# Attention in a fused kernel: the short query block of 64 rows moves from the end to the start

## The chip, the cores and the metric

The kernel runs on one core of a Trainium2 chip. The metric is the device time of one execution in microseconds (us). The program computes causal attention, a mixture of experts and a gated MLP in one launch; the change touches only the attention.

## What is computed

```python
scores = q @ k.T / sqrt(64)                       # 4 batches x 8 heads, S = 576, D = 64
cum    = cumsum(maximum(s, 0))
scores = where(causal, -1e9, scores + minimum(-(cum[:, None] - cum[None, :]), 0))
p      = exp(scores - rowmax(scores))
out    = (p / (p.sum(-1) + 1e-9)) @ v
x      = out as 2304 tokens x 512                  # then: top-1 of 8 experts, 512 -> 1024 -> 512
y      = (silu(norm(x) @ w_gate) * (norm(x) @ w_val)) @ w_out      # 512 -> 1536 -> 512
```

The term that depends on the row alone falls out of a softmax, so the kernel adds only the column's cumulative sum, less the one in the middle. Everything is float32.

## The kernel before

**Pairs.** The 32 heads are handled as 16 pairs, p0 to p15. The two heads of a pair lie on the upper and the lower 64 rows of TensorE's array, so their matmuls run side by side.

**Query blocks.** A pair has five blocks of queries. Blocks 0 to 3 hold 128 queries each and see 128, 256, 384 and 512 columns of keys for each head (`s_start`, `s_mm`). Block 4 holds the last 64 queries of both heads, one head above the other on 128 partitions; a block-diagonal copy of q (`q_diag`, L284, on GpSimd) makes that one matmul, over 576 keys in two halves of 288 (L341).

**Steps of a pair.** TensorE writes scores into PSUM (tiles `s` and `sm`). VectorE reads them, adds the bias, scales, and takes the row's extreme in one pass (`reduced`, L298). ScalarE takes the exponential with the row sums (`s_exp`, L354). TensorE transposes the probabilities in 25 squares of 128 x 128, seven groups t0 to t6 (`t_mm`, L373), ScalarE copies them to `pt` (L406), and TensorE multiplies by v (`pv_mm`: `pvy` L419, `pvx` L423) and, with the gate's weights, forms the output tile `tl` (`o_mm`, L447). PSUM has eight banks in one rotation, shared by all of these tiles: a tile waits until the reader of the eighth tile before it is done.

**Bias.** `load_bias` sends each pair's cumulative sums to all partitions by DMA: `sums`, two transfers of 256 KB, and `cm`, two of 144 KB, for the block of two heads. From p2 on the causal mask is not a matmul but part of the bias, and GpSimd prepares it (`mask_sums`): once per pair for both heads (n = 0: L249 and L250, 512 and 256 columns) and, once VectorE has read block 1, once for each head (n = 1, 2: L253, 256 columns each), into the same buffer. Block 2 is reduced after that, as the last of the four wide ones (`TURN`).

**Order.** A list `plan` holds the steps with a key 10*p + POS. TensorE, ScalarE, VectorE and SyncE take them in the order of the keys. GpSimd does not: its order is made by the framework's planner, which takes what it reckons to be ready and, of several ready ones, the earlier in the program. `in_turn` adds explicit orders: what it wraps comes after the last instruction in `k.turn`. The program order of `mask_sums` is

```python
S=[0.11, 0.2, 0.81, 0.83, 5.96],      # keys of the five score steps, in the order TURN
MASK = -9.7                           # mask_sums(p + 1, 0) stands at 10 * p + 0.3
mask_sums(k, p, 1 + h)                # inside s_mm(p, 1), so at 10 * p + 0.2
```

so `mask_sums(p + 1, 0)` follows `mask_sums(p, 1)` and `(p, 2)`, and is tied behind them by `in_turn`. SyncE issues the loads of q, k, bias and v for later pairs, and from p1 to p3 the eight `prefill` transfers, which write filler rows to the experts' token buffer (`xs<-zrow`).

Of the kernel before, what the change touches and what calls it, by code (L numbers as in the profile page):

```python
# [2063 lines left out]
```

## Time and profile before

| | us |
|---|---|
| median of three runs (838.82 to 839.22) | 839.19 |
| the profiled execution | 838.61 |
| its span | 836.9 |
| TensorE busy | 816.7 (98%) |
| VectorE busy | 639.6 (76%) |
| ScalarE busy | 461.9 (55%) |
| GpSimd busy | 227.0 (27%) |

The span runs from the first to the last instruction. In the views PE is TensorE, DVE is VectorE, ACT is ScalarE, POOL is GpSimd and SP is SyncE; L298 is line 298 of the kernel, and PEclk is the granted clock of TensorE, with 1.00 for 2.4 GHz and 0.50 for 1.2 GHz. The attention fills about 5 to 180 us; a pair begins with its first `s` matmul and takes about 10.4 us, while its later steps overlap the next pairs.

### The profile page before, as it was taken

What the parts mean: (1) busy time and instruction counts of PE and PEld (TensorE: products, weight loads), DVE (VectorE), ACT (ScalarE), POOL (GpSimd) and SP (SyncE); (2) the same over time, 40 slices, a digit from 0 to 9 for tenths busy, and PEclk for the clock granted to TensorE, in tenths of its full rate; (3) what the DMA queues carried; (4) which work ended last, traced back from release to release, by engine and by line L of the source; (5) the groups of instructions that cost most, each with busy time, mean ns of one, the idle gap of its engine ahead of it and who ended that gap; (6) DMA issues with size and microseconds to landing.
All of it is one profiled execution on the core that took longest, in us unless ns stands there. A gap on an engine that the chain in (4) does not pass through costs nothing.

```text
span 836.9 us, 15788 instructions
## 1 busy us (share of the span) xinstructions
PE 816.7 (98%) x5622; PEld 746.7 (89%) x5622; DVE 639.6 (76%) x1425; ACT 461.9 (55%) x1060; POOL 227.0 (27%) x249
## 2 busy tenths in 40 slices
PE   7999999999999999999999999999999999999994
PEld 4777767789899999999999999999999998899994
DVE  6657688965866768777698988988888869868880
ACT  5988989865756656566543433333333334553440
POOL 3335856332000000000221233444343351031120
PEclk9999999999999999999999999999999999999997
DMA  7999989236567566767661332322222376344510
GB/s 226 299 320 314 315 245 295 84 126 214 193 193 245 179 228 204 237 206 233 225 197 66 131 109 103 131 94 98 104 100 99 108 282 191 81 151 146 159 52 29
DMA packets 79757, 146.72 MB, mean 175 GB/s; under 512 B 7424, under 2 KB 44315, under 8 KB 79667
## 3 DMA queue, kind: packets, MB, share of 16 engines
q1 hardware_dynamic: 76707, 136.08, 51.4%
q0 software_dynamic: 2912, 9.46, 3.0%
q8 instruction: 46, 0.75, 0.4%
q14 instruction: 44, 0.36, 0.1%
q10 hardware_dynamic: 48, 0.07, 0.0%
HBM read 108.04 MB, written 37.54 MB: 174 GB/s over the span
## 4 chain that ended last, share of the span: by engine, by line
PE 92%; DVE 3%; ACT 2%; DMA 1%; issue 1%; SPq 0%; POOL 0%; POOLq 0%; DVEq 0%; ACTq 0%
PE gg L1320 29%; PE g L938 12%; PE g L915 12%; PE gp L1778 10%; PE go L1713 6%; PE pvy L419 5%; PE t L373 5%; PE s L310 5%; PE tl L447 2%; PE sm L341 1%; PE xp L886 1%; ACT pt L406 1%; DMA ringa<-ytd 1%; PE r L987 1%; PE r L976 1%
## 5 line engine op out<-in xcount | busy, mean ns | idle before, releaser
L938 PE MATMUL g<-h,u 128*128 128x256 f32 (+7 forms) x768 | 104.3, 294 | 0.0
L915 PE MATMUL g<-xt,u 128*128 128x256 f32 (+7 forms) x768 | 103.9, 294 | 0.0
L915 PEld LDWEIGHTS g<-xt,u 128*128 128x128 f32 x768 | 101.0, 188 | 0.8
L938 PEld LDWEIGHTS g<-h,u 128*128 128x128 f32 x768 | 100.5, 188 | 0.5
L1297 POOL TENSOR_TENSOR ws<-raw,ws 128x512 fp32r<-128x512 f32 (+1 forms) x25 | 33.0, 1335 | 219.4 <-ACT ws L1292 219.4
L747 ACT CAST u<-raw 128x1024 fp32r<-128x1024 f32 x62 | 65.1, 1050 | 20.9 <-DMA raw<-in_w 20.9
L354 ACT ACTIVATE p<-sc,nm 128x128 f32<-128x128 f32 (+3 forms) x128 | 71.2, 581 | 6.0 <-DVE nm L298 6.0
L760 DVE TENSOR_TENSOR u<-raw,u 128x1024 fp32r<-128x1024 f32 x58 | 70.3, 1216 | 0.9 <-ACT u L747 0.9
L1320 PE MATMUL gg<-gx2a,ws 128*128 128x384 f32 x360 | 67.4, 335 | 0.6 <-DVE tmp L1342 0.6
L1320 PE MATMUL gg<-gx0a,ws 128*128 128x384 f32 x360 | 67.7, 336 | 0.0
L1320 PE MATMUL gg<-gx1a,ws 128*128 128x384 f32 x360 | 67.1, 335 | 0.0
L1320 PEld LDWEIGHTS gg<-gx2a,ws 128*128 128x128 f32 x360 | 62.8, 188 | 0.9 <-DVE tmp L1342 0.9
L1320 PEld LDWEIGHTS gg<-gx0a,ws 128*128 128x128 f32 x360 | 63.1, 188 | 0.0
L1320 PEld LDWEIGHTS gg<-gx1a,ws 128*128 128x128 f32 x360 | 62.7, 188 | 0.0
L1358 POOL TENSOR_TENSOR hs<-tmp,hs 128x384 f32<-128x384 f32 x27 | 30.3, 1122 | 106.2 <-ACT hs L1356 106.2
L406 ACT COPY pt<-t 128x512 f32<-128x512 f32 (+3 forms) x160 | 56.0, 451 | 3.0 <-PE t L373 2.0
L373 PE MATMUL t<-ident,p 128*128 128x128 f32 x400 | 52.1, 275 | 0.1
L373 PEld LDWEIGHTS t<-ident,p 128*128 128x128 f32 x400 | 44.5, 140 | 8.5 <-DVE nm L298 8.3
L1699 POOL DMA_INDIRECT out<-raw,oid x18 | 20.5, 1138 | 112.1 <-DVE raw L1800 64.5
L419 PE MATMUL pvy<-pt,vp 128*64 128x512 f32 (+4 forms) x320 | 47.5, 428 | 0.9 <-ACT pt L406 0.9
L1338 ACT COPY tmp<-gg 128x384 f32<-128x384 f32 x27 | 13.0, 482 | 57.1 <-PE gg L1320 55.4
L1248 ACT ACTIVATE raw<-raw 128x512 f32<-128x512 f32 x31 | 21.1, 681 | 36.0 <-DVE raw L1246 35.8
(391 smaller groups left out, 1809.5 us busy)
## 6 DMA issues: line engine op xcount, KB each, us to landing
raw<-in_w SPq DMA_DIRECT2D x64, 512.0 KB
hd<-hs SPq DMA_DIRECT2D x72, 192.0 KB
xs<-zrow SPq DMA_DIRECT2D x8, 771.0 KB
raw<-in_wo SPq DMA_DIRECT2D x12, 512.0 KB
raw<-in_wg SPq DMA_DIRECT2D x12, 512.0 KB
...
in<-cumd SPq DMA_DIRECT2D x20, 256.0 KB
```

Source lines behind the costliest of these rows:

```text
L310: k.nc.tensor.matmul(ps[h], st.q[r, 128 * i:128 * i + 128], st.k[r, 0:w], start=True, stop=p >= BYPE)
L354: k.nc.scalar.activation(out, st.s[i, h][:, 0:w], AF.Exp, bias=st.nm[:, n:n + 1], scale=-1.0, accum_out=acc)
L373: nc.tensor.transpose(ps[:, off:off + 128], src[:, 128 * j:128 * j + 128], k.ident)
L406: nc.scalar.copy(b, a)
L419: nc.tensor.matmul(st.y[r, a - 64:512], st.v[:, h, j, :], k.pt[:, h, o:o + S - a], start=j == 0, stop=j == 4)
L747: nc.scalar.copy(w[:, :, 0, :], raw)
L760: k.nc.vector.tensor_tensor(w[:, :, 1, :], raw, w[:, :, 0, :].bitcast(F32), op=ALU.subtract)
L915: nc.tensor.matmul(ps[:, 0:n], w[:, f % 4, a, 128 * kc:128 * kc + 128], x[b][:, kc, 0:n], start=kc == 0 and i == 0, stop=kc == 3 and i == 2)
L938: nc.tensor.matmul(ps[:, 0:n], w[:, f % 4, a, 128 * c:128 * c + 128], k.h[b][:, f, 0:n], start=f == 0 and i == 0, stop=f == 7 and i == 2)
L1320: k.nc.tensor.matmul(k.ps[u, bank], w[:, a, 128 * c:128 * c + 128], x[:, b, GT * c:GT * c + GT], start=first and c == 0 and n == 0, stop=c ...
L1713: k.nc.tensor.matmul(k.acc[tau], c[:, a, 128 * t:128 * t + 128], w[:, b, :], start=f == 0 and i == 0, stop=f == NF - 1 and i == 2)
L1778: k.nc.tensor.matmul(k.acc[i, bank], t[:, a, j, :], item_weight(k, j, w, b), start=first and j == 0 and n == 0, stop=j == 5 and n == 2, sk ...
```

## The change

Block 0 is now the short one: the first 64 queries of both heads, merged, which see only the first 64 keys. Blocks 1 to 4 hold 128 queries each and see 192, 320, 448 and 576 columns for each head; block 4 is computed in two halves of 288, the right one first. The order of the blocks becomes 1, 2, 4, 3, 0. The transposes stay 25 squares: where before three of a pair's squares came from the merged block alone, now a square can hold the last 64 columns of one head beside the first 64 of the other, with `h = 1` stored in reversed units of 64 (v is laid out to match). The copies to `pt` stay ten, over the same number of columns; the spare parts of `pt` are set to zero once at the start in place of two other pads.

`mask_sums` works in units of 64 columns: 384, 512 and 256 columns in three instructions for n = 0, and 128 columns in place for each head for n = 1 and 2. These two now stand inside `s_mm(p, 4)`, whose key is 10*p + 0.81, and block 3 reads what they write. `load_bias` sends `sums` as two transfers of 288 KB and `cm` as two of 16 KB. The constants `mz`, `half` and `zrow` move into unused parts of other buffers. The first two score steps of p0 that start ahead of the bias are blocks 1 and 2.

The core of the diff (`consts`, `route` and the places that only rename are left out):

```diff
     k.identb = P.tile([128, 128], BF16, name="identb")
-    k.mz = P.tile([128, 2, 128], F32, name="mz")
+    k.mz = k.pp[0][:, 3328:3584]
     nc.gpsimd.memset(k.mz, 0.0)
-    mk = k.mz[:, 0, :]
...
-    for i in range(2):
+    for i in (1, 2):
         s_start(k, 0, i)
...
 
 
 HALF = S // 2
...
-SPLIT = ((0, 576), (576, 1152), (1152, 2688), (2688, 3264), (3264, 3392))
+PTW = 1984
+STRIP = (1408, 0, 448, 896, 1344)
+START_OF = [128 * i * i - 128 for i in range(5)]
+UNITS64, C0, LAST = 16, 4, 13
+
...
-    for n in range(2):
-        nc.gpsimd.memset(k.pvt[n][:, S:640], 0.0)
-        p = pp[n]
-        nc.gpsimd.memset(p[:, 2560 + S:3200], 0.0)
-        q = [[p[:, 1280 * h + 64 * i * (i + 1):1280 * h + 64 * (i + 1) * (i + 2)] for h in range(2)] for i in range(4)]
-        k.p.append((q, p[:, 2560:3200]))
+    for p in pp:
+        k.p.append((p, p[:, 3072:3136]))
     k.pt = slot(k, 2, [2, PTW], name="pt")
+    for a in STRIP:
+        for h in range(2):
+            nc.gpsimd.memset(k.pt[64 - 64 * h:128 - 64 * h, h, a:a + 64], 0.0)
     sm = A.tile([128, 2], F32, name="sm")
     k.sm, k.rs = [sm[:, n:n + 1] for n in range(2)], []
...
+        u = 4 - a
+        if len(out.shape) == 4:
+            return G.tensor_tensor(out, src, mz[:, a:4].unsqueeze(1).broadcast_to((128, 2, u, 64)), op=ALU.add)
+        return G.tensor_tensor(out, src, mz[:, a:4], op=ALU.add)
+
     if n == 0:
-        m = k.mz[:, 0, :].unsqueeze(1)
-        in_turn(k, G.tensor_tensor(cb[:, :, 0:2, :], cb[:, :, 3:1:-1, :], m.unsqueeze(1).broadcast_to(sh), op=ALU.add))
-        in_turn(k, G.tensor_tensor(cb[:, :, 5, :], cb[:, :, 5, :], m.broadcast_to((128, 2, 128)), op=ALU.add))
+        in_turn(k, add(cb[:, :, LAST:16, :], cb[:, :, C0:C0 + 3, :], 1))
+        in_turn(k, add(cb[:, :, C0 - 1::-1, :], cb[:, :, C0 + 1:C0 + 5, :], 0))
+        in_turn(k, add(cb[:, :, C0 + 7:LAST, :], cb[:, :, C0 + 7:LAST, :], 2))
     else:
-        h = n - 1
-        k.turn = [G.tensor_tensor(cb[:, h, 0:2, :], cb[:, h, 4:2:-1, :], k.mz, op=ALU.add).ins]
+        c = cb[:, n - 1, C0 + 5:C0 + 7, :]
+        k.turn = [add(c, c, 2).ins]
 
...
     for h in range(2):
-        k.nc.sync.dma_start(out=sums(st, h)[:, c:512], in_=k.cumd[2 * p + h:2 * p + h + 1, c:512].broadcast_to((128, 512 - c)))
+        k.nc.sync.dma_start(out=sums(st, h)[:, c:S], in_=k.cumd[2 * p + h:2 * p + h + 1, c:S].broadcast_to((128, S - c)))
     for h in range(2):
-        k.nc.sync.dma_start(out=st.cm[64 * h:64 * h + 64, :], in_=k.cumd[2 * p + h:2 * p + h + 1, :].broadcast_to((64, S)))
+        k.nc.sync.dma_start(out=st.cm[64 * h:64 * h + 64, :], in_=k.cumd[2 * p + h:2 * p + h + 1, 0:64].broadcast_to((64, 64)))
...
-def s_start(k, p, i):
-    st, w = k.st[p], 128 * (i + 1)
-    ps = st.ps[i] = [k.psum.tile([128, 512], F32, name=f"s{p}_{i}_{h}", tag="b")[:, 0:w] for h in range(2)]
+def width(i):
+    return 64 + 128 * i
...
+def s_start(k, p, i, c=0, w=None):
+    st, w = k.st[p], w or width(i)
+    q = slice(128 * i - 64, 128 * i + 64)
+    ps = st.ps[i, c] = [bank(k, f"s{p}_{i}_{c}_{h}", w) for h in range(2)]
     for h, r in enumerate(ROWS2):
-        k.nc.tensor.matmul(ps[h], st.q[r, 128 * i:128 * i + 128], st.k[r, 0:w], start=True, stop=p >= BYPE)
+        k.nc.tensor.matmul(ps[h], st.q[r, q], st.k[r, c:c + w], start=True, stop=p >= BYPE or c + w < width(i))
...
-        if i not in st.ps:
+        ps = bank(k, f"sm{p}", 64)
+        nc.tensor.matmul(ps, st.bd, st.k[:, 0:64], start=True, stop=False)
+        nc.tensor.matmul(ps, k.identb, k.mask[:, 0, 0:64], start=False, stop=True)
+        reduced(k, scores(0)[:, 0:64], ps, st.cm, acc(10))
...
+        if (i, 0) not in st.ps:
             s_start(k, p, i)
-        ps = st.ps.pop(i)
-        for n in range(2 if p < BYPE else 0):
...
+        if p < BYPE:
+            mask_pe(k, ps, w)
         for h in range(2):
-            sc = st.s[i, h] = A.tile([128, S], F32, name=f"sc{p}_{i}_{h}", tag="sc", bufs=4)
-            acc = st.nm[:, 2 * i + h:2 * i + h + 1]
-            if p < BYPE:
-                reduced(k, sc[:, 0:w], ps[h], sums(st, h)[:, 0:w], acc)
+            sc, a = scores(h)[:, 0:w], acc(2 * i - 2 + h)
+            c = st.cb[:, h]
+            if p < BYPE or i == 3:
+                reduced(k, sc, ps[h], sums(st, h)[:, 0:w], a)
+            elif i == 1:
+                reduced(k, sc, ps[h], flat(c[:, LAST:16, :]), a)
             else:
-                reduced(k, *(t.rearrange("p (b n) -> p b n", n=128) for t in (sc[:, 0:w], ps[h])), bias_of(st, i, h), acc)
...
+    else:
+        for c in (HALF, 0):
+            s_start(k, p, 4, c, HALF)
+        if p < BYPE:
+            mask_pe(k, st.ps[4, HALF], HALF)
+        sc = [scores(h) for h in range(2)]
+        for c in (HALF, 0):
+            ps = st.ps.pop((4, c))
+            for h in range(2):
+                reduced(k, sc[h][:, c:c + HALF], ps[h], sums(st, h)[:, c:c + HALF], acc((8 if c else 6) + h))
+                if c and p >= BYPE:
                     mask_sums(k, p, 1 + h)
-    else:
...
-    out = ph[i][h] if i < 4 else pm[:, 0:S]
-    acc = k.rs[p % 2][:, i, h:h + 1] if i < 4 else k.sm[p % 2]
-    k.nc.scalar.activation(out, st.s[i, h][:, 0:w], AF.Exp, bias=st.nm[:, n:n + 1], scale=-1.0, accum_out=acc)
+    i, h = (0, 0) if n == 8 else (n // 2 + 1, n % 2)
+    w = width(i)
+    out, src = pm, st.s[i, h][:, 0:w]
+    if i:
+        a = START_OF[i] + w * h
+        out = ph[:, a:a + w]
+        if h:
+            out, src = (t.rearrange("p (b n) -> p b n", n=64) for t in (out, src))
+            out = out[:, ::-1, :]
+    acc = k.rs[p % 2][:, i, h:h + 1] if i else k.sm[p % 2]
+    at = n if i else 10
+    k.nc.scalar.activation(out, src, AF.Exp, bias=st.nm[:, at:at + 1], scale=-1.0, accum_out=acc)
...
     ev = []
-    if g < 2:
...
+        j, h = divmod(g, 2)
+        for i in range(j + 1, 5):
+            tr(128 * (i - j - 1), i, h, j)
+        n = 512 - 128 * j
+        a = STRIP[j] + 64
+        ev.append((ps[:, 0:n], pt[:, h, a:a + n]))
...
-        for j in range(2):
-            tr(256 + 128 * j, pm, j)
-        ev.append(both(0, 2, JB[3]))
-        ev.append((ps[:, 256:512].rearrange("p (j h n) -> p h j n", j=2, h=2),
-                   k.pt[:, :, 512:512 + 896].rearrange("p h (j c) -> p h j c", j=2)[:, :, :, 0:64]))
+            tr(128 * h, 4, h, 3)
+        nc.tensor.transpose(ps[0:64, 256:384], pm, k.ident)
+        ev.append((both(0, 128), pt[:, :, STRIP[3] + 64:STRIP[3] + 192]))
+        for h in range(2):
+            ev.append((ps[0:64, 256 + 64 * h:320 + 64 * h], pt[64 * h:64 * h + 64, h, STRIP[0]:STRIP[0] + 64]))
     else:
-        for j in range(2, 5):
-            tr(128 * (j - 2), pm, j)
-        for j in range(2, 5):
-            ev.append(both(128 * (j - 2), 1, JB[j] + 512 - 128 * j))
+        for i in range(1, 5):
+            a = START_OF[i] + 128 * i
+            nc.tensor.transpose(ps[:, 128 * i - 128:128 * i], ph[:, a:a + 128], k.ident)
+        for h in range(2):
+            ev.append((ps[64 * h:64 * h + 64, :].rearrange("p (i n) -> p i n", i=4)[:, :, 64:128],
+                       pt[64 * h:64 * h + 64, h, 0:1792].rearrange("p (i n) -> p i n", i=4)[:, :, 0:64]))
...
-TURN = dict(S=(0, 1, 3, 2, 4), X=(0, 1, 2, 3, 6, 7, 4, 5, 8))
+TURN = dict(S=(1, 2, 4, 3, 0), X=(0, 1, 2, 3, 6, 7, 4, 5, 8))
```

## Rows read from the trace of the kernel before

**Rows 1.** The chain that ended last, of the whole span: share by engine.

```profile
PE 92%; DVE 3%; ACT 2%; DMA 1%; issue 1%; SPq 0%; POOL 0%; POOLq 0%; DVEq 0%; ACTq 0%
```

**Rows 2.** PE timeline of pair 4 and the start of pairs 5 and 6: start, duration (us).

```profile
43.76 2.43 PE L310 MATMUL s<-in,in 64*128 64x128 f32 x16
...
48.63 0.93 PE L373 MATMUL t<-ident,p 128*128 128x128 f32 x7
...
49.89 1.13 PE L341 MATMUL sm<-in,p 128*128 128x288 f32 x4
50.86 0.19 PE L343 MATMUL sm<-mask,identb 128*128 128x64 bf16 x1
...
52.22 0.28 PE L423 MATMUL pvx<-pt,vp 128*64 128x64 f32 x4
52.33 1.90 PE L419 MATMUL pvy<-pt,vp 128*64 128x448 f32 x16
54.16 2.43 PE L310 MATMUL s<-in 64*128 64x128 f32 x16
...
59.19 0.93 PE L373 MATMUL t<-ident,p 128*128 128x128 f32 x7
...
64.72 1.78 PE L310 MATMUL s<-in 64*128 64x128 f32 x12
```

**Rows 3.** Windows of ordinary, busy and long stretches: length, busy time, PEclk, DMA share, GB/s.

```profile
43.76:54.16 10.40, 10.40 (x84) 7.50 (x80) 6.52 (x29) 9.43 (x30) 2.12 (x4) 1.00 1.06 314
...
86.40:97.17 10.77, 10.47 (x84) 7.51 (x80) 6.62 (x29) 10.12 (x29) 9.86 (x9) 1.00 0.98 354
97.17:108.02 10.85, 10.48 (x85) 7.51 (x81) 6.59 (x31) 10.85 (x35) 8.46 (x7) 1.00 1.01 290
...
10.00:100.00 90.00, 89.23 (x693) 62.53 (x690) 59.05 (x273) 82.07 (x268) 39.98 (x47) 1.00 1.03 313
```

**Rows 4.** POOL timeline of the pairs 3 to 6: start, duration, idle before, releaser.

```profile
35.01 1.42 POOL L253 TENSOR_TENSOR in<-in,mz 128x256 f32<-128x256 f32 x2 [4.92 <-DVE nm L298]
...
42.04 1.28 POOL L249 TENSOR_TENSOR cb<-cb,mz 128x512 f32<-128x512 f32 x1 [2.27 <-DMA cb<-cumd]
43.27 0.73 POOL L250 TENSOR_TENSOR cb<-cb,mz 128x256 f32<-128x256 f32 x1
45.42 1.42 POOL L253 TENSOR_TENSOR cb<-cb,mz 128x256 f32<-128x256 f32 x2 [1.42 <-DVE nm L298]
...
54.67 1.26 POOL L249 TENSOR_TENSOR in<-in,mz 128x512 f32<-128x512 f32 x1 [2.15 <-DMA in<-cumd]
...
65.10 1.27 POOL L249 TENSOR_TENSOR in<-in,mz 128x512 f32<-128x512 f32 x1 [6.70 <-DMA in<-cumd]
...
67.01 0.47 POOL L284 TENSOR_TENSOR in<-in,half 128x128 f32<-128x128 f32 x1
```

**Rows 5.** VectorE lines by form, 20 to 180 us: two reduces, mean ns, idle time, releasers.

```profile
L298 DVE CUSTOM_DVE_ANT_1 sc<-s,in 128x384 f32<-128x384 f32 x20 | 10.3, 553 | 0.0
...
L298 DVE CUSTOM_DVE_ANT_0 sc<-s,in 128x128 f32<-128x128 f32 x20 | 5.0, 288 | 11.5 <-PE s L310 8.9 <-POOL in L249 2.6
```

**Rows 6.** DMA issues of the whole span: count and KB of each.

```profile
in<-cumd SPq DMA_DIRECT2D x20, 256.0 KB
...
in<-cumd SPq DMA_DIRECT2D x22, 144.0 KB
```

**Rows 7.** Windows of the last stretches: granted clock after the last matmul.

```profile
820.00:825.00 5.00, 4.66 (x41) 4.45 (x40) 0.73 (x2) 0.37 (x1) 0.98 (x1) 1.00 0.06 16
825.00:830.00 5.00, 0.00 (x0) 0.00 (x0) 0.12 (x1) 0.00 (x0) 0.98 (x1) 0.74 0.30 105
830.00:836.90 6.90, 0.00 (x0) 0.00 (x0) 0.00 (x0) 0.00 (x0) 0.00 (x0) 0.50 0.00 1
```

**Rows 8.** PE timeline of the start: equal scores of pair 0 and pair 1.

```profile
9.11 2.06 PE L310 MATMUL s<-in 64*128 64x512 f32 x4
...
14.49 1.11 PE L310 MATMUL s<-in,in 64*128 64x512 f32 x4
```

More of the change, by code (lines that the diff above doesn't have):

```diff
@@ L94, in masks @@
     nc, P = k.nc, k.apool
+    k.pp = [slot(k, n, [4096], name=f"p{n}") for n in range(2)]
     k.identb = P.tile([128, 128], BF16, name="identb")
-    k.mz = P.tile([128, 2, 128], F32, name="mz")
+    k.mz = k.pp[0][:, 3328:3584]
     nc.gpsimd.memset(k.mz, 0.0)
-    mk = k.mz[:, 0, :]
+    mk = k.mz[:, 128:256]
     nc.gpsimd.affine_select(out=mk, in_=mk, compare_op=ALU.is_ge, fill=NEG, base=0,
                             pattern=[[-1, 128]], channel_multiplier=1)
-    k.half = P.tile([128, 2, 64], F32, name="half")
+    k.half = k.pp[0][:, 3584:3712].rearrange("p (h n) -> p h n", h=2)
     nc.gpsimd.memset(k.half, 0.0)
@@ L303, with bank, mask_pe @@
 BYPE = 2
-def s_start(k, p, i):
-    st, w = k.st[p], 128 * (i + 1)
-    ps = st.ps[i] = [k.psum.tile([128, 512], F32, name=f"s{p}_{i}_{h}", tag="b")[:, 0:w] for h in range(2)]
-    for h, r in enumerate(ROWS2):
-        k.nc.tensor.matmul(ps[h], st.q[r, 128 * i:128 * i + 128], st.k[r, 0:w], start=True, stop=p >= BYPE)
+def width(i):
+    return 64 + 128 * i
+def bank(k, name, w):
+    return k.psum.tile([128, 512], F32, name=name, tag="b")[:, 0:w]
+def s_start(k, p, i, c=0, w=None):
+    st, w = k.st[p], w or width(i)
+    q = slice(128 * i - 64, 128 * i + 64)
+    ps = st.ps[i, c] = [bank(k, f"s{p}_{i}_{c}_{h}", w) for h in range(2)]
+    for h, r in enumerate(ROWS2):
+        k.nc.tensor.matmul(ps[h], st.q[r, q], st.k[r, c:c + w], start=True, stop=p >= BYPE or c + w < width(i))
+def mask_pe(k, ps, w):
+    for n in range(2):
+        for h, r in enumerate(ROWS2):
+            k.nc.tensor.matmul(ps[h][:, w - 128 + 64 * n:w], k.pick[r, n, :], k.mask[r, n, 64 * n:128],
+                               start=False, stop=n == 1)
 def s_mm(k, p, i):
@@ new lines, in scores, with acc @@
+    def scores(h):
+        sc = st.s[i, h] = A.tile([128, S], F32, name=f"sc{p}_{i}_{h}", tag="sc", bufs=4)
+        return sc
+    def acc(n):
+        return st.nm[:, n:n + 1]
+    if i == 1:
+        st.nm = A.tile([128, 12], F32, name=f"nm{p}", tag="nm", bufs=3)
+    w = width(i)
+    if i == 0:
+        ps = bank(k, f"sm{p}", 64)
+        nc.tensor.matmul(ps, st.bd, st.k[:, 0:64], start=True, stop=False)
+        nc.tensor.matmul(ps, k.identb, k.mask[:, 0, 0:64], start=False, stop=True)
+        reduced(k, scores(0)[:, 0:64], ps, st.cm, acc(10))
+    elif i < 4:
+        if (i, 0) not in st.ps:
+            s_start(k, p, i)
+        ps = st.ps.pop((i, 0))
+        if p < BYPE:
+            mask_pe(k, ps, w)
+        for h in range(2):
+            sc, a = scores(h)[:, 0:w], acc(2 * i - 2 + h)
[4 more added lines that the diff above has]
+                reduced(k, sc, ps[h], flat(c[:, LAST:16, :]), a)
+            else:
+                reduced(k, *(t.rearrange("p (b n) -> p b n", n=64) for t in (sc, ps[h])), c[:, C0::-1, :], a)
+    else:
[9 more added lines that the diff above has]
+                if c and p >= BYPE:
+                    mask_sums(k, p, 1 + h)
+        nc.vector.tensor_tensor(st.nm[:, 6:8], st.nm[:, 6:8], st.nm[:, 8:10], op=ALU.min)
@@ L367, in t_mm, with tr @@
 def t_mm(k, p, g):
-    nc = k.nc
+    nc, pt = k.nc, k.pt
     ph, pm = k.p[p % 2]
     ps = k.psum.tile([128, 512], F32, name=f"t{p}_{g}", tag="b")
-    def tr(off, src, j):
-        nc.tensor.transpose(ps[:, off:off + 128], src[:, 128 * j:128 * j + 128], k.ident)
-    def both(a, j, n):
-        return ps[:, a:a + 128 * j].rearrange("p (h n) -> p h n", h=2), k.pt[:, :, n:n + 64 * j]
-    ev = []
-    if g < 2:
-        for i in range(4):
-            tr(128 * i, ph[i][g], 0)
-        ev.append((ps, k.pt[:, g, 0:512]))
-    elif g < 4:
-        for i in range(1, 4):
-            tr(128 * (i - 1), ph[i][g - 2], 1)
-        ev.append((ps[:, 0:384], k.pt[:, g - 2, JB[1]:JB[1] + 384]))
+    def tr(off, i, h, j):
+        a = START_OF[i] + (width(i) + 64 * (2 * i - 2 * j - 1) if h else 128 * j)
+        nc.tensor.transpose(ps[:, off:off + 128], ph[:, a:a + 128], k.ident)
@@ L387, in t_mm, with both @@
+    def both(a, n):
+        return ps[:, a:a + 2 * n].rearrange("p (h n) -> p h n", h=2)
+    ev = []
+    if g < 4:
+        j, h = divmod(g, 2)
[4 more added lines that the diff above has]
+        ev.append((ps[:, 0:n], pt[:, h, a:a + n]))
     elif g == 4:
         for h in range(2):
-            for i in range(2, 4):
-                tr(256 * h + 128 * (i - 2), ph[i][h], 2)
-        ev.append(both(0, 4, JB[2]))
+            for i in (3, 4):
+                tr(256 * h + 128 * (i - 3), i, h, 2)
+        ev.append((both(0, 256), pt[:, :, STRIP[2] + 64:STRIP[2] + 320]))
@@ L422, in pv_mm @@
             r = slice(64 * h, 64 * h + 64)
-            nc.tensor.matmul(st.xp[r, :], st.v[:, h, 0, :], k.pt[:, h, 0:64], start=True, stop=True)
+            nc.tensor.matmul(st.xp[r, :], st.v[:, h, 0, :], k.pt[:, h, STRIP[0]:STRIP[0] + 64], start=True, stop=True)
 def pv_out(k, p, i):
@@ L446, in o_mm @@
         st.o = k.psum.tile([128, nt, 144], F32, name=f"tl{p}_{t0}", tag="b")
-    nc.tensor.matmul(st.o[:, i - t0, :], k.pvt[p % 2][:, 128 * i:128 * i + 128], k.tg[:, h0 // 2, :], start=True, stop=True)
+    nc.tensor.matmul(st.o[:, i - t0, :], k.pvt[p % 2][:, max(128 * i - 64, 0):max(128 * i - 64, 0) + 128], k.tg[:, h0 // 2, :], start=True, stop=True)
     if i in (2, 4):
```

60 lines of the change are left out of this document (21 added, 39 removed).

## The prediction

> **What bounds the kernel now.** I read the chain of waits first: TensorE holds 92% of it [rows 1], so a change counts by what it does to TensorE's own work, or by the gaps it opens there. Second, TensorE's timeline of one pair: scores begin at 43.76 and the next pair's at 54.16, 10.40 us without a visible gap [rows 2]. Third, windows of whole pairs: TensorE is busy 10.40 of 10.40, ScalarE 9.43; in two pairs with extra work ScalarE is busy 10.12 of 10.77 and 10.85 of 10.85, so there it sets the pace [rows 3]. The same view gives the DMA engines as fully busy from 10 to 100 us, at 313 GB/s. Last, GpSimd's timeline, because the bias comes through it: its first mask sum of p6 begins at 65.10 after 6.70 us of waiting for the bias's DMA, and that of p4 at 42.04, p5 at 54.67, each released by a DMA [rows 4]. The scores of p5 begin at 54.16 and those of p6 at 64.72 [rows 2], so the bias of the next pair lands about 11 us into a pair that lasts 10.5: it is just in time. VectorE has already waited 2.6 us in all for those sums [rows 5].
>
> **The change part by part.** *Matmul columns.* The wide blocks grow from 1280 to 1536 columns a head, +256; a float32 matmul takes two passes. The merged block before takes four passes of 288 from 49.89 to 50.86, 0.97 us for 1152 columns, 0.84 ns a column [rows 2]. So the scores gain 256 x 2 x 0.84 = 0.43 us a pair (heads lie side by side). The merged block falls from 0.97 us to two passes of 64; `pvx` with four such instructions takes 0.11 us, 52.22 to 52.33 [rows 2], and I take 0.11. That is -0.86, together -0.43 us a pair. Transposes, copies to `pt`, the products with v and the output tiles keep their counts and columns: 0.
>
> *How much of it counts.* In the fourteen pairs from p2 on, twelve are set by TensorE: 12 x 0.43. In the two that ScalarE fills [rows 3] I take 0.1 each, since the exponentials keep count and columns. In p0 and p1, where the start is set by loads, reduces and exponentials, I take 0. Without any new wait this is 5.36 us.
>
> *Loads.* `cm` goes from 2 x 144 KB to 2 x 16 KB, `sums` from 2 x 256 to 2 x 288 [rows 6]: 256 KB less, at 313 GB/s 0.84 us, and 64 KB more, 0.21; net 0.63 us a pair of a saturated queue. Six pairs' loads lie ahead of p6's `sums`, whose own add 0.21: its first sum starts at 65.10 - 6 x 0.63 + 0.21 = 61.5; where the early ones are no gain, up to 62.2. By the same count p4's starts at 39.7 and p5's at 51.7.
>
> The DMA engines show this in their row as bytes only: no run so far times rows of 256 B, which the new `cm` has. The Trainium skill, DMA: Bandwidth & Descriptors, Specifications, asks for at least 512 B in a transfer for line rate; by it the new `cm` would cost like rows of 512 B, an estimate of 0.1 us more a pair, and the bias of p6 would come 0.6 us later, the total 0.6 higher.
>
> *The order on GpSimd.* This is the part that decides. Before, the sums for each head of p5 follow block 1 and come ahead of p6's sums by an explicit order. Now they stand later in the program than p6's sums, and nothing ties them: the instruction that waits for p6's DMA may stand at the head of GpSimd's queue, with the sums that p5's block 3 needs behind it. The planner's choice is seen in the rows only for another pair of instructions: the sums of p6 (65.10) went ahead of p6's `q_diag` (67.01), as in the program, while waiting 6.70 us for a DMA [rows 4]. It believes the DMA earlier than it is. So I take program order for p6.
>
> *What that costs.* After the DMA, p6's three sums take 384 + 512 + 256 columns: 1.24 us for 512 (42.04 to 43.27), 0.68 for 256 (two in 1.42) [rows 4], about 0.96 for 384: 2.9. The sum for p5's first head, 128 columns, is 0.46 (as `q_diag`, 67.01) [rows 4]; its block 3, 448 columns, lies above the 384-column reduce of 553 ns [rows 5], about 0.62. With semaphores: 4.1 us. Who waits: `s_3` of p5 fills the two banks that the transposes t5 and t6 of p4 take eight tiles later, and TensorE runs in order, so all its work stands behind t5. t5 begins at 61.5 + 4.1 = 65.6, against 59.19 before, which is 54.16 + 5.03 [rows 2].
>
> From t5 to the next scores lie 64.72 - 59.19 = 5.53 us before [rows 2], now less 0.86: 4.67. So p6's scores begin at 70.3 instead of 64.72: +5.6 us. It does not matter whether p4's and p5's sums also go first: then the t5 that runs beside p3 waits until 39.7 + 4.1 = 43.8, the one beside p4 until 55.8, p5's scores begin at 55.8 + 4.7 = 60.5, and t5 of p4 stands at 60.5 + 5.03 + 0.43 = 66.0, within half a us of the same. I add 0.3 for ScalarE, which has 1 us of air in a pair [rows 3] and must catch up. What is late next is p7's bias, which the queue goes on bringing during the stall, so p6 waits no more. From p6 on the ten pairs give back, two of them the ones that ScalarE fills: 8 x 0.43 + 2 x 0.1 = 3.6.
>
> Sum against the profiled execution, 838.61: +5.6 + 0.3 - 3.6 = +2.3, or 840.9. The median is 0.58 above that execution: 841.5.
>
> *Costs at nothing.* The ten memsets of `pt`, the wider loads of p0 and the moved constants are hidden by the start, where GpSimd and TensorE wait for loads; if p0's block 2 (whose last 64 columns now come by DMA) were late, it costs up to 1 us. SyncE's issue count is the same. ScalarE's last exponential and the merged block are shorter for t5: no gain while TensorE sets the pace.
>
> **The rivals.**
> (a) *No stall.* The planner puts p5's head sums first. For it: it does order by its own times, and lighter loads do not make p6's bias later. Against: 65.10 before 67.01. Then 839.19 - 5.36 = 833.8.
>
> (b) *The stall and a slow clock*: slower than before by more. TensorE would idle up to 6 us in one piece. The granted clock was 1.00 while TensorE worked (820 to 825), 0.74 in the next 5 us with nothing on TensorE, 0.50 after [rows 7]: it fell within an idle of 5 us. At the start, at the lower level, four 512-column score instructions took 2.06 us against 1.11 later [rows 8]; the low level held for about 4.4 us of work (from 5.2 to about 9.7), so a fall costs about 2.2: 843.7. It decides where the idle is one piece, as it is after 825 us, that is where only p6's sums go first; if p3's, p4's and p5's go first too, the idle is split over three pairs, and what a fall costs in one is eaten by the next wait.
>
> The Trainium skill, TensorE: Matmul & The Clock Gate, What's actually happening, says that throttled is the default and activity releases it; the rows agree with both directions, and by it each restart after a long stall pays as the start did, which is (b) once more.
>
> (c) *The stall is shorter.* p6's bias comes earlier than by bytes, or t5 needs less than 4.1 us: each us less is 1 us, so 838 to 840.5.
>
> **How the numbers follow.** The stall without loss of clock 0.45, around 841.5 (840 to 843); (b) 0.25, around 843.7; (a) 0.2, 833.8; (c) 0.1. One in ten of (a) could lie below 833, one in six of (b) above 845.5. The range is 833.0 to 845.5. A difference of 0.2%, 1.7 us, is what a measurement can tell: below 837.5 lie (a) and most of (c), 0.27; from 837.5 to 840.9 the lower third of the main case and the rest of (c), 0.22; above, 0.51.
>
> **What would show it.** In the changed kernel: GpSimd's instruction of p6's sums, waiting for the DMA at about 61.5, with the 128-column sums of p5 behind it, and t5's row on TensorE at about 65.6 after idle time released by VectorE; p6's scores at about 70.3; pairs of 9.97 us from p10 on. If the 128-column sums stand ahead, the stall step is wrong and (a) holds; if PEclk falls below 1.00 in the pairs p4 to p6, (b). If pairs without extra work still take 10.4 us, the column sum is wrong.

## The result, and the profile after

The changed kernel takes 846.34 us (median of 5, 844.35 to 847.72) against 839.19 (838.48 to 840.25) in the same rounds: ratio 1.0077 [1.0066, 1.0089], slower. The forecast was 841.5, slower, with a range up to 845.5. The profiled execution has a span of 844.6 us against 836.9: +7.7.

The chain of waits, which came first in the forecast, is of little use here: in the changed kernel's trace it can be followed back only to 697.57 us. TensorE's starts of the scores show the place instead (rows of its timeline, read off for p0 and for p2 to p15; under them the length of each stretch):

```
before  5.22 23.44 33.35 43.76 54.16 64.72 75.99 86.40  97.17 108.02 118.99 130.28 140.69 151.10 162.10
         18.22  9.91 10.41 10.41 10.56 11.26 10.41 10.78  10.84  10.97  11.29  10.41  10.41  11.00
after   5.30 24.75 34.64 47.17 58.94 68.98 79.91 89.94 101.02 112.45 127.74 139.35 149.38 159.86 170.78
         19.45  9.89 12.53 11.78 10.03 10.93 10.03 11.08  11.44  15.29  11.61  10.03  10.48  10.92
```

The account, after less before: p0 and p1 +1.23; p2 0; p3 and p4 +2.12 and +1.37; p5 to p7 -0.53, -0.33, -0.38; p8 and p9 +0.30 and +0.60; p10 +4.32; p11 to p14 together -0.07; from p15's scores to the end -0.98. An ordinary pair is 10.03 for 10.41. Three places lose: p3/p4, p8/p9 with the start, and p10.

**p3 and p4: GpSimd's order.** GpSimd's timeline of the changed kernel (start, duration, idle before and what ended it), answering [rows 4]; the last two lines are those that matter for p10. L257 is the next pair's three mask sums, L258 the two head sums that block 3 needs:

```profile
38.12 2.91 POOL L257 TENSOR_TENSOR cb<-cb,p 128x384 f32<-128x384 f32 x3 [7.86 <-DMA cb<-cumd]
40.98 0.87 POOL L258 TENSOR_TENSOR in<-in,p 128x128 f32<-128x128 f32 x2
...
49.86 2.95 POOL L257 TENSOR_TENSOR in<-in,p 128x384 f32<-128x384 f32 x3 [7.47 <-DMA in<-cumd]
52.76 0.87 POOL L258 TENSOR_TENSOR cb<-cb,p 128x128 f32<-128x128 f32 x2
...
58.98 2.92 POOL L257 TENSOR_TENSOR in<-in,p 128x384 f32<-128x384 f32 x3 [4.81 <-DMA in<-cumd]
61.88 0.87 POOL L258 TENSOR_TENSOR in<-in,p 128x128 f32<-128x128 f32 x2
...
107.78 2.91 POOL L257 TENSOR_TENSOR in<-in,p 128x384 f32<-128x384 f32 x3 [2.22 <-DMA in<-cumd]
110.64 4.86 POOL L795 TENSOR_TENSOR u<-raw,u 128x1024 fp32r<-128x1024 f32 x2
```

The next pair's sums stand ahead and wait for the DMA, 7.86 and 7.47 us; the head sums, which need no DMA any more, stand behind. TensorE's timeline, answering [rows 2], shows who pays (first two lines, t5 released by VectorE's reduce), and p10 in the last three:

```profile
42.16 0.44 PE L419 MATMUL t<-ident,p 128*128 128x128 f32 x2 [1.64 <-DVE nm L306]
...
53.94 0.44 PE L419 MATMUL t<-ident,p 128*128 128x128 f32 x2 [1.31 <-DVE nm L306]
...
112.45 2.10 PE L327 MATMUL s<-in,in 64*128 64x192 f32 x14
116.84 1.50 PE L327 MATMUL s<-in,in 64*128 64x288 f32 x6 [2.29 <-DVE nm L306]
118.28 2.49 PE L419 MATMUL t<-ident,p 128*128 128x128 f32 x11
```

The loads are the forecast's (DMA issues, answering [rows 6]):

```profile
in<-cumd SPq DMA_DIRECT2D x20, 288.0 KB
...
in<-cumd SPq DMA_DIRECT2D x22, 16.0 KB
```

VectorE's idle time is put on the same instruction; the group answers to [rows 5], where it waited for L249 (form | busy, mean ns | idle before and releaser):

```profile
L306 DVE CUSTOM_DVE_ANT_0 sc<-s,in 128x448 f32<-128x448 f32 x20 | 11.6, 616 | 2.4 <-POOL in L258 2.3
```

**p10: VectorE held while GpSimd runs.** Beside the attention the kernel prepares weights of the later stages in pieces. For a piece of the experts' weights ScalarE makes a cast (L793) and GpSimd the difference (L795), at the keys `PIECES`; for a piece of the out-weights VectorE works on raw bits (L1291 to L1293). VectorE's timeline of the changed kernel: the key puts the first piece of the out-weights ahead of the reduces of p10's block 1.

```profile
111.45 0.23 DVE L306 CUSTOM_DVE_ANT_0 sc<-sm,in 128x64 f32<-128x64 f32 x1 [3.71 <-ACT p L399]
...
112.19 1.11 DVE L1291 TENSOR_SCALAR raw<-raw 128x512 uint32<-128x512 uint32 x1
113.33 2.72 DVE L1292 SCALAR_TENSOR_TENSOR raw<-raw 128x512 uint32<-128x512 uint32 x1
116.09 0.43 DVE L1293 TENSOR_SCALAR raw<-raw 128x512 uint32<-128x512 uint32 x1
116.43 0.35 DVE L306 CUSTOM_DVE_ANT_0 sc<-s,cb 128x192 f32<-128x192 f32 x1
```

In the kernel before, the same two instructions, on VectorE, began after GpSimd's two pieces (second fence: L749, 102.68 to 107.37) had ended:

```profile
107.90 0.42 DVE L1245 TENSOR_SCALAR raw<-raw 128x512 uint32<-128x512 uint32 x1
108.35 0.70 DVE L1246 SCALAR_TENSOR_TENSOR raw<-raw 128x512 uint32<-128x512 uint32 x1
```

```profile
102.68 4.69 POOL L749 TENSOR_TENSOR u<-raw,u 128x1024 fp32r<-128x1024 f32 x2
```

So 0.42 became 1.11, and 0.70 became 2.72, while L795 ran from 110.64 to 115.50; L1292 ends 0.55 us after L795. The pieces run later because L257 of p11 stands ahead of them on GpSimd, waiting for its DMA until 107.78. The reduce inside the same stretch (111.45, input in PSUM) keeps its 0.23. The Trainium skill, SBUF — State Buffer, Who interferes with whom, says that VectorE and GpSimd share one pair of ports, taken whole for an instruction by whoever issued first, and that a VectorE instruction with two SBUF inputs, or a tensor_scalar in a two-port mode, needs it. The trace agrees in both instructions, and in the reduce that is not held; that L1291 runs in such a mode no row here says.

What the 2.29 us of idle TensorE do next is seen in windows (length, then busy time of PE, PEld, DVE, ACT, POOL; PEclk, DMA share, GB/s), answering [rows 3]: an ordinary pair, two stretches that hold the stalls of p3 and p4, p9, p10, and the part of p10 at the lower clock.

```profile
58.94:68.98 10.04, 10.04 (x87) 7.51 (x83) 7.21 (x31) 9.59 (x30) 7.09 (x9) 1.00 0.94 323
...
40.00:50.00 10.00, 8.36 (x66) 5.35 (x64) 5.13 (x25) 8.02 (x27) 2.46 (x6) 1.00 1.05 335
50.00:60.00 10.00, 8.69 (x74) 6.52 (x74) 5.46 (x24) 8.04 (x24) 5.11 (x8) 1.00 1.01 318
...
101.02:112.45 11.43, 11.20 (x84) 8.33 (x82) 6.51 (x32) 11.30 (x33) 6.56 (x8) 1.00 0.91 315
112.45:127.74 15.29, 13.00 (x94) 9.59 (x93) 13.94 (x45) 10.97 (x34) 7.27 (x8) 0.89 0.39 114
...
118.45:121.86 3.41, 3.41 (x17) 3.40 (x17) 3.33 (x14) 2.10 (x5) 3.33 (x5) 0.50 0.03 7
```

In p10 the granted clock falls: eleven transposes at 118.28 take 2.49 us for the usual 1.42, and TensorE is busy 13.00, where p10 of before was busy 10.97 of 10.97. So its +4.32 is 2.29 of waiting and 2.03 more of busy time. The 3.41 us at 0.50 account for at most half their length, 1.7. What the rest is was not shown; in e1 and e10 p10 is busy 0.8 longer too, at 1.00. In the split stalls of p3 and p4 the clock stays at 1.00 in this run; in c2 below, the same kernel on another chip, it did not.

**p8, p9 and the start: ScalarE.** p9 is filled by ScalarE, 11.30 of 11.43, as before it was 10.85 of 10.85. Its copies to `pt` by form (x, busy, mean ns), after:

```profile
L452 ACT COPY pt<-t 64x256 f32<-64x256 f32 x30 | 11.0, 367 | 0.7
L452 ACT COPY pt<-t 64x64 f32<-64x64 f32 x30 | 6.2, 207 | 0.4
L452 ACT COPY pt<-t 128x256 f32<-128x256 f32 x15 | 5.7, 381 | 3.4 <-PE t L440 3.4
```

and the whole row of ten copies in p0, after, then before (ScalarE's timeline):

```profile
19.15 3.67 ACT L452 COPY pt<-t 128x512 f32<-128x512 f32 x10
```

```profile
17.71 3.31 ACT L406 COPY pt<-t 128x512 f32<-128x512 f32 x10
```

To the next instruction these are 3.69 and 3.17 us, though the count is ten in both: +0.52 a pair, hidden where TensorE sets the pace.

### The profile page after: what moved, and what is told of

Read it like the earlier page. It is cut to its first block, busy times and chain, and to the rows that moved or that the text cites. A ratio compares the mean times of both kernels' runs of the same rounds, so it can differ in the third digit from the quotient of the medians.

```text
span 844.6 us, 15907 instructions
## 1 busy us (share of the span) xinstructions
PE 819.7 (97%) x5654; PEld 752.5 (89%) x5654; DVE 645.9 (76%) x1457; ACT 468.7 (55%) x1060; POOL 235.2 (28%) x270
## 5 line engine op out<-in xcount | busy, mean ns | idle before, releaser
L399 ACT ACTIVATE p<-sc,nm 128x192 f32<-128x192 f32 (+2 forms) x144 | 82.7, 577 | 5.9 <-DVE nm L306 3.7
L793 ACT CAST u<-raw 128x1024 fp32r<-128x1024 f32 x62 | 65.0, 1048 | 21.4 <-DMA raw<-in_w 21.3
L452 ACT COPY pt<-t 128x512 f32<-128x512 f32 (+4 forms) x160 | 60.3, 429 | 9.6 <-PE t L419 4.9
L306 DVE CUSTOM_DVE_ANT_0 sc<-s,in 128x288 f32<-128x288 f32 (+3 forms) x90 | 38.3, 470 | 16.0 <-PE s L327 6.1
L465 PE MATMUL pvy<-pt,vp 128*64 128x448 f32 (+4 forms) x320 | 48.9, 429 | 0.2
L419 PEld LDWEIGHTS t<-ident,p 128*128 128x128 f32 x320 | 37.2, 144 | 13.2 <-DVE nm L306 11.1
L419 PE MATMUL t<-ident,p 128*128 128x128 f32 x320 | 44.8, 282 | 3.2 <-DVE nm L306 3.2
```

Source lines behind the costliest of these rows:

```text
L306: k.nc.vector.tensor_tensor_reduce(out=out, in0=ps, in1=bias, scale=-0.125, scalar=3e38, op0=ALU.add, op1=ALU.min, accum_out=accum)
L399: k.nc.scalar.activation(out, src, AF.Exp, bias=st.nm[:, at:at + 1], scale=-1.0, accum_out=acc)
L419: nc.tensor.transpose(ps[:, off:off + 128], ph[:, a:a + 128], k.ident)
L452: nc.scalar.copy(b, a)
L465: nc.tensor.matmul(st.y[r, a - 64:512], st.v[:, h, j, :], k.pt[:, h, o:o + S - a], start=j == 0, stop=j == 4)
L793: nc.scalar.copy(w[:, :, 0, :], raw)
```

## The experiments

Theory: three separate causes, (A) GpSimd's order in p3/p4, (B) VectorE's raw-bit instructions held by GpSimd in p10, (C) the copies onto 64 partitions. Rivals: the new loads or the new matmuls themselves are slow; or p10 is only the echo of p3/p4. The chips differ: the kernel before takes 839 to 841 us on two of them and 845 to 847 on three, so every ratio is to the kernel before on the same chip.

**e1_order**, A alone removed (next sums behind the head sums):

```diff
-MASK = -9.7
+MASK = -9.18
```

> The changed kernel with one edit: the sums for the next pair's bias are issued after the two sums for each head and tied behind them, as before the change. Theory A: the order on GpSimd is behind both large losses, the waits of t5 in p3 and p4 (about 4.3 us against ordinary pairs) and the 4.7 us in p10, where the late sums of p11 push GpSimd's weight pieces into VectorE's ones. Then S of p5 begins at about 54.9, p10 takes about 10.5, and the time is 837 to 838. Rival B: p10's loss comes with ScalarE's later schedule, not with the order; then only the first 4.3 go, and the time is about 842. Rival C: the order is no cause; 846.

847.05 against 845.13, 1.0014 [1.0000, 1.0028]. GpSimd's timeline of this run:

```profile
37.68 0.88 POOL L258 TENSOR_TENSOR in<-in,p 128x128 f32<-128x128 f32 x2 [5.62 <-DVE nm L306]
38.63 2.92 POOL L257 TENSOR_TENSOR cb<-cb,p 128x384 f32<-128x384 f32 x3
...
47.99 0.88 POOL L258 TENSOR_TENSOR cb<-cb,p 128x128 f32<-128x128 f32 x2 [6.03 <-DVE nm L306]
50.64 2.93 POOL L257 TENSOR_TENSOR in<-in,p 128x384 f32<-128x384 f32 x3 [1.77 <-DMA in<-cumd]
```

The two waits of t5 are gone, p3 10.32, p4 10.03, p5 10.07. p10 still takes 12.80, so it is no echo of p3/p4; it had been expected at 10.5 and the time at 837 to 838, 1 to 2 under the kernel before. The order is thus only a part of p10's loss. GpSimd in p9 of this run, the head sums and then its two weight pieces, and under it the head sums of p9 in the kernel before:

```profile
101.38 0.88 POOL L258 TENSOR_TENSOR in<-in,p 128x128 f32<-128x128 f32 x2 [2.45 <-DVE nm L306]
...
105.64 4.67 POOL L795 TENSOR_TENSOR u<-raw,u 128x1024 fp32r<-128x1024 f32 x2
```

```profile
98.83 1.43 POOL L253 TENSOR_TENSOR in<-in,mz 128x256 f32<-128x256 f32 x2 [2.21 <-DVE nm L298]
```

The head sums now follow the right half of block 4 and begin 3.20 us after p9's scores (98.18), before 1.66 (97.17). With the order restored the pieces still end 0.70 after p10's scores begin (109.61); before they ended 0.65 ahead of them. There L1291 takes 1.25 instead of 0.42, and L1292 again 0.69.

**e2_order_low, e3_order_high**, the changed kernel's order left only in p8 and later, or only before p8:

```diff
-                add(10 * p + MASK, mask_sums, k, p, 0)
+                add(10 * p + (-9.18 if p < 8 else MASK), mask_sums, k, p, 0)   # e2
+                add(10 * p + (-9.18 if p >= 8 else MASK), mask_sums, k, p, 0)  # e3
```

> The changed kernel with the old order only for the sums of p3 to p7. Theory A: t5 no longer waits in p3 and p4, p10 still loses its 4 to 5 us: 841.5 to 842.5. Rival B says the same here. Rival C: 846.

> The changed kernel with the old order only for the sums of p8 to p15. Theory A: the waits in p3 and p4 stay, p10 falls from 15.3 to about 10.5 us: 841 to 842. Rival B: p10 stays at 15.3, 846.

e2: 850.65, 1.0055 [1.0032, 1.0077], p3 10.03 and p10 13.98, L1292 again 2.73. e3: 852.28, 1.0077 [1.0054, 1.0101], p3 12.18, p4 14.44, p10 12.70. Each place is lost without the other. As repairs both miss what was expected. e3's ratio is that of the changed kernel on the first chip; on its own chip the changed kernel was not run. Its p4 holds a fall of the clock (0.88 over the pair).

**e4_before_early**, the kernel BEFORE with nothing but the order on GpSimd turned round:

```diff
-MASK = -9.7
+MASK = -9.85
```

> The kernel before with one edit: the sums of the next pair stand ahead of the two sums for each head in the program, and are not tied behind them; everything else as before. Theory A: the wait for a bias stands ahead of what block 2 needs. By the landing of p6's bias at 65.1, two sums of 1.92, a head's sum of 0.7 and a reduce of 0.6, t5 beside p5 waits until 68.3 instead of 59.2, and the time is 846 to 852, the upper end with a fall of the clock. Rival C, that the order costs nothing by itself: 839.

857.35 against 845.13, 1.0135 [1.0112, 1.0159]; p5 20.91. GpSimd, TensorE, and the windows of this run:

```profile
67.24 1.26 POOL L249 TENSOR_TENSOR in<-in,mz 128x512 f32<-128x512 f32 x1 [7.77 <-DMA in<-cumd]
...
69.14 0.72 POOL L253 TENSOR_TENSOR in<-in,mz 128x256 f32<-128x256 f32 x1
```

```profile
70.52 0.90 PE L373 MATMUL t<-ident,p 128*128 128x128 f32 x3 [7.96 <-DVE nm L298]
```

```profile
62.50:70.50 8.00, 0.06 (x1) 0.00 (x0) 0.60 (x3) 0.70 (x3) 3.08 (x4) 0.67 0.98 269
70.50:75.00 4.50, 4.48 (x16) 3.45 (x18) 2.00 (x11) 3.30 (x11) 1.52 (x2) 0.50 1.01 286
```

The order alone makes the stall, with the old loads and the old matmuls: A is shown from both sides. p3 and p4 show none here (10.41 each). The pair loses 10.50 (20.91 for 10.41), of it 7.96 waiting and 2.5 at the lower clock, which stayed at 0.50 (1.2 GHz) for 4.5 us.

**c1_before, c2_after, c3_before**, the two kernels unchanged on other chips, for stretches to compare with.

> The kernel before, unchanged, for its trace on the chip of these runs. In the last four runs the kernel before took 845.1 us, 6 more than where the prediction was made, and PE's results in p12 were signalled 3 us late in all four kernels. If that belongs to the chip, p12 takes 12 us or more here too; if it comes from the edits, p12 takes 10.4.

> The changed kernel, unchanged, to stand beside the next two on one chip: 7 us over the kernel before, with the waits of t5 in p3 and p4 and the loss in p10.

> The kernel before, unchanged, for its trace on the chip of the next two. If the loss of 3 to 6 us in p12 belongs to a chip and not to the edits, a chip on which the kernel before takes 845 us or more shows it here too; on a chip where it takes 839 to 841, p12 takes 10.4.

c1 839.7, its start 19.26. c2 851.92, 1.0118 [1.0089, 1.0147], p3 12.50, p4 14.67, p10 17.93: the loss has the same places and is larger. TensorE's wait in p4, and the window of that pair:

```profile
55.27 0.47 PE L419 MATMUL t<-ident,p 128*128 128x128 f32 x2 [2.74 <-DVE nm L306]
```

```profile
47.06:61.74 14.68, 11.94 (x87) 8.77 (x83) 6.26 (x31) 10.43 (x34) 5.63 (x8) 0.88 1.01 339
```

Here the granted clock fell in p4, the sign that the forecast had named for its rival (b), after a wait twice that of the first run (2.74 for 1.31): p5's bias landed at 51.21, 4.15 us into the pair, where it had been 2.69.

c3 846.1 with p12 14.09: the kernel before loses 3.7 us in p12 on that chip too, so this much is not of the change. e1, on another slow chip, took 16.10 there; no trace of the kernel before from that chip stands beside it.

**e5_decode, e6_both**, VectorE's three instructions of the first piece moved behind p10's reduces; e6 is that with e1's edit:

```diff
-            add(at + (7.25 if n == 1 else 6.3), out_first, k, 4 + n)
+            add(at + (11.0 if n == 0 else 7.25 if n == 1 else 6.3), out_first, k, 4 + n)
```

> The changed kernel with one edit: VectorE's first three instructions on a piece of the out weight are issued after p10's reduces instead of ahead of them; the order of the bias sums stays as changed. Theory A with its second half, that these instructions cannot run while GpSimd works on its weight pieces: they no longer hold up p10's scores, p10 falls from 15.3 to about 10.5 and the time by 4 to 5 us, to about 2.5 over the kernel before. Rival: p10's loss comes with the lag of ScalarE; then p10 stays near 15 and the time at 7 over.

> The changed kernel with both edits: the sums of the next pair behind those for each head, and VectorE's three instructions after p10's reduces. Theory A: both large losses go, what is left is the later start (+1.3), p8 and p9 (+0.9) and 0.38 gained in each of ten pairs: 1 to 2 us under the kernel before. Rival: the losses return at another place, and it is not below the kernel before.

e5: 847.45, 1.0083 [1.0055, 1.0112], 4.5 less than c2; p10 13.43, p3 and p4 still long (15.46, with a fall of the clock, and 11.25). e6: 843.06, 1.0024 [1.0015, 1.0034], 4.4 less again; p3 10.03, p4 10.07, p10 13.68, where now a routing matmul waits 2.18 for VectorE. So the steps for (B) and for (A) each gain, but the p10 loss moves on with the VectorE instructions that are moved, and e6 misses the 1 to 2 us under the kernel before that were expected.

**e10_before_late**, B put into the kernel BEFORE (two pieces of GpSimd's splitting 2.2 and 2.4 later in the plan):

```diff
-PIECES = (81.8, 84.0, 91.8, 94.0, 159.0, 161.7)
+PIECES = (81.8, 84.0, 94.0, 96.4, 159.0, 161.7)
```

> The kernel before with one edit: the two weight pieces of p9 stand later, at 94.0 and 96.4 instead of 91.8 and 94.0, so that GpSimd works on the second one until about 110.9. Theory: VectorE's instructions on the out weight, at 107.9, wait for GpSimd's to end, p10's reduces follow late, TensorE waits about 2.5 us, and the time is 2 to 5 us over the kernel before, with everything of the change left out. Rival, that VectorE is not held by GpSimd: within 1 us of the kernel before.

846.9 against 846.08, 1.0017 [1.0001, 1.0033]. GpSimd, then VectorE, in this run:

```profile
108.75 2.62 POOL L749 TENSOR_TENSOR u<-raw,u 128x1024 fp32r<-128x1024 f32 x1 [0.92 <-ACT u L747]
```

```profile
109.19 2.72 DVE L1246 SCALAR_TENSOR_TENSOR raw<-raw 128x512 uint32<-128x512 uint32 x1
```

Where the two meet, the 0.70 become 2.72 in the old kernel as well, again ending 0.5 us after GpSimd's: that VectorE is held is shown. The price is smaller than expected: p10 takes 12.65 for 10.97, of it 0.86 is TensorE's wait for VectorE, p9 takes 10.41 for 10.84, and the total moves by 0.8, not 2 to 5.

**e7_spread, e8_copies, e9_start**: e1's edit with the pieces further apart (e7); with two of the 64-partition copies on VectorE (e8); with p0's blocks in another order (e9):

```diff
+PIECES = (71.8, 81.8, 84.0, 91.8, 159.0, 161.7)      # e7, e8, e9
+        if g == 5 and n:                             # e8
+            nc.vector.tensor_copy(b, a)
+TURN_0 = dict(S=(1, 2, 3, 4, 0), ...)                # e9, used for p0
```

> The changed kernel with the sums of the next pair behind those for each head, and with the four weight pieces (ScalarE's cast and GpSimd's difference) in p7, p8, p8 and p9 instead of two in p8 and two in p9; VectorE's instructions on the out weight stay at their place. Theory: the collision in p10 needs GpSimd still at work on the last piece when p10 starts; now it ends about 2 us earlier, p10 takes about 11 us instead of 12.8 to 13.7, and p9, with one cast less on ScalarE, 10.3 instead of 11.4. The time is 2 us under the kernel before. Rival, that p10's loss comes from a late ScalarE and not from GpSimd: p10 stays over 12 and the time within 1 us of the kernel before or over it.

> As the kernel with the spread pieces, and the two copies of 64 columns onto 64 partitions in t5's group on VectorE instead of ScalarE. Theory: on ScalarE a copy onto one half of the partitions does not overlap its neighbours (0.25 and 0.23 us a copy, together 0.48 of the 0.52 by which the ten copies of a pair grew), and this is felt where ScalarE sets the pace, in p0, p1 and p8: about 1 us less than the kernel with the spread pieces alone. Rival, that ScalarE's copies are hidden: no difference, or slower where VectorE's copy waits behind its reduces.

> As the kernel with the spread pieces, and p0 alone takes its blocks in the order 1, 2, 3, 4, 0 with the exponentials in that order. Theory: at the start ScalarE waits 1.67 us for block 4, whose row extreme needs four reduces; block 3 needs one for each head. ScalarE's first copies to pt begin about 1 us earlier, and the time falls by 0.5 to 1 us against the spread pieces alone. Rival: the start is bound by the slow clock of TensorE, and nothing changes.

e7: 846.32, 1.0003 [0.9992, 1.0013], p10 11.66, as fast as before, not the 2 us faster that were expected. e8: 848.42, 1.0039 [1.0023, 1.0055]; the start is 19.04 for 19.44, p7 10.04 for 10.32, p8 11.35 for 11.74, which is C's sign, but p10 to p14 lost 2.1, more than was gained: a miss in the total. e9: 847.1, 1.0011 [1.0001, 1.0021]; p0 20.61, worse by 1.2: a miss.

**e11 to e15**, looking for a version that keeps the gain. In e7, VectorE's two-column minimum (L383) takes 619 ns, since L257 now runs beside it. e11 ties L257 behind the reciprocal of the normalisation; e12 adds e8's copies up to p8, and the three after it keep them; e13, e14 and e15 vary which pairs are tied so, and the pieces (edits shortened):

```diff
-    nc.vector.reciprocal(st.r, st.r)
+    k.turn = k.turn + [nc.vector.reciprocal(st.r, st.r).ins]   # e11 to e15; e11, e12 with MASK -8.99
+PIECES = (71.8, 81.8, 91.8, 101.8, 159.0, 161.7)                # e11, e12
+PIECES = (71.8, 77.5, 84.0, 91.8, 159.0, 161.7)                 # e13, e14
+PIECES = (71.8, 81.8, 84.0, 91.8, 159.0, 161.7)                 # e15
+ -9.18 if p == 10 else -8.99 if p < 12 else -9.7                # e13, e15; e14: no p < 12
```

> The changed kernel with the next pair's sums behind the normalisation on VectorE (tied to its last instruction), and with one weight piece in each of p7 to p10. Theory: block 4's minimum falls from 0.68 us in the mean to about 0.2, no pair but p8 to p10 is over 10.1 us, and these take 10.4 to 10.9 for ScalarE's cast and its slower copies; the time is 2 to 3 us under the kernel before. Rival: the small losses are ScalarE's, and it is level with the kernel before.

> As the last, with the two copies of 64 columns onto 64 partitions on VectorE for the pairs before p9. Theory: 0.4 less in each of p0, p7 and p8, and nothing lost later: 1 us under the last. Rival: level with it.

> The changed kernel with the next pair's sums behind the normalisation for p2 to p11 (for p10 right behind the sums for each head), at the changed kernel's own place for p12 to p15; the weight pieces two in p7, one in p8, one in p9; the two short copies on VectorE for the pairs before p9. Theory, that p10's loss is GpSimd's piece meeting VectorE's long-waiting instructions: p10 takes 10.5 to 11.3, and the time is 2 to 3 us under the kernel before. Rival: p10 stays over 12.5 and the time level with the kernel before.

> As e13, with the sums of p12 to p15 behind the normalisation too. Theory: in p11 and p14 they meet the routing's short instructions on VectorE, 1 to 1.5 us more than e13. Rival: no difference.

> As e13, with one piece in p7, two in p8 and one in p9. Within 0.5 us of e13: ScalarE's extra cast costs about 0.5 to 1 us in whichever pair holds two.

In e11 the short VectorE instructions are free again (lines by form, 20 to 105 us; in e7 541 and 619):

```profile
L408 DVE TENSOR_SCALAR r<-rs 128x10 f32<-128x10 f32 x9 | 1.6, 174 | 0.3
L383 DVE TENSOR_TENSOR nm<-nm 128x2 f32<-128x2 f32 x8 | 1.4, 170 | 0.3
```

but p10 takes 16.02: 848.83, 1.0020 [1.0006, 1.0035]. e12: 846.98, 1.0003 [0.9990, 1.0016]; p10 begins at 105.68, 4.4 us ahead of c3 (1.5 of it lost in c3's own p8, 12.31), and gives it back (p10 16.00, p11 12.73). e13: 843.19, 1.0032 [1.0021, 1.0043]. e14: 844.34, 1.0040 [1.0026, 1.0054]. e15: 842.37, 1.0022 [1.0011, 1.0033]; p10 begins at 106.18, 2.8 ahead of c1, and takes 14.21. VectorE, GpSimd and TensorE in p10 of e13:

```profile
114.43 1.13 DVE L1298 TENSOR_SCALAR raw<-raw 128x512 f32<-128x512 f32 x1
115.59 1.66 DVE L1299 SCALAR_TENSOR_TENSOR raw<-raw 128x512 uint32<-128x512 uint32 x1
...
119.19 1.30 DVE L550 TENSOR_TENSOR eq<-eq,w8v 128x40 f32<-128x40 f32 x1
```

```profile
114.27 3.57 POOL L257 TENSOR_TENSOR in<-in,p 128x384 f32<-128x384 f32 x3 [2.35 <-issue]
...
118.22 2.89 POOL L257 TENSOR_TENSOR in<-in,p 128x384 f32<-128x384 f32 x3
```

```profile
121.22 0.19 PE L561 MATMUL rk<-oh,tri 128*128 128x40 bf16 x1 [3.02 <-DVE oh L555]
```

In the kernel before, the instructions of these three VectorE rows take 0.42, 0.83 and 0.19. In e6 and in all five of these, TensorE waits in p10 at the next matmul that needs VectorE's chain for the routing (1.5 to 3.4 us). No version tried beats the kernel before; e11, e12 and e13 missed the 2 to 4 us under it that were expected. Whether some placement keeps the gain is open: from p2's scores to p10's e12 takes 81.5 us, the kernel before 84.6. So is why the slower chips lose time in p12.

## Why the prediction was wrong

| step | forecast | measured |
|---|---|---|
| ordinary pair | -0.43 | -0.38 |
| bias of p4, p5, p6 | 39.7, 51.7, 61.5 | 38.12, 49.86, 58.98 |
| from there to t5 | 4.1 | 4.04, 4.08, no wait for p6 |
| scores of p6 | +5.6 | +4.26 |
| ScalarE catching up | +0.3 | not seen |
| p6 to the end | -3.6 | +3.4 |

*Right.* The direction, and the step said to decide: GpSimd kept program order, t5 waited for a DMA of another pair, in the form "p3's, p4's and p5's go first too", and what remained of the stall was the forecast's own 4.1 us behind the landing. e1 and e4 show the cause. Rival (b)'s condition was right for p3 to p6 in this run: the idle came in pieces and the clock held. In c2, with the same order, it fell in p4. Its price for one fall, 2.2, was 2.5 in e4, but the reading behind it was wrong: by [rows 8] the instructions at 9.11 still ran at the lower level, so that lasted to about 11.2 and not to 9.7. That the price came near is luck. The list of chances also puts most of (c) below 837.5, while (c) itself says 838 to 840.5.

*Mis-sized.* The bias came 1.6, 1.8 and 2.5 us earlier than the bytes gave, so p6's cost nothing. At p6's scores +4.26 stood for +5.6, and 1.23 of that is the start, which the forecast had at 0: the stalls cost 3.0, 2.6 less than forecast. The queue had moved 332 GB/s from 20 us to the landing of p6's bias (58.98), where the kernel before moved 308 to its own (65.10); why it moved more was not tried. Rows of 256 B show no cost that would have delayed it. By the rule cited in the forecast (the Trainium skill, DMA: Bandwidth & Descriptors, Specifications) it would have come later than that count.

*Wrong, the step that failed*: "From p6 on the ten pairs give back, two of them the ones that ScalarE fills: 8 x 0.43 + 2 x 0.1 = 3.6." They cost 3.4. Of the 7.0 us between, 4.75 are p10 (+4.32 for -0.43): the forecast asked for TensorE alone who waits for GpSimd's late sums, and not what else stands behind them on GpSimd, and which VectorE instructions that meets; with the old order (e1) p10 still loses 1.8, as the head sums themselves moved later in the pair and the weight pieces behind them still reach into it. With the pieces placed earlier (e7) it takes 11.66. 1.1 are p8 and p9 (+0.90 for -0.2): "exponentials keep count and columns" was true, but the copies kept their count and columns too and still cost 0.52 more a pair. The rest, 1.2, is p6, p7 and p11 on, where the gain is only partly kept.

*Also wrong by a part*: p0 and p1 at 0, measured +1.23. The kernel before itself takes 19.26 and 19.16 there in c1 and c3 instead of 18.22, so at most 0.3 of it is steadily the change's. In c1 the lower clock lasts longer: block 2's four matmuls at 11.11 take 1.63, in the first trace 1.13. The changed kernel takes 19.44 or 19.45 with a late rise of the clock (c2) or an early one (e1). In both ScalarE waits 1.67 us for block 4's extreme, but e9, meant to shorten that wait, made the start worse, so what sets it is not shown. e8's 0.4 says that the copies are part of it. Rival (a), no stall, failed as said; with the order kept, the time is 1.0014 of before (e1) and not 5.4 us less.
